# Folding the last four weight rows of the upper 64 partitions onto the lower 64, in the tail of a decode kernel

## Chip, cores and metric

The kernel runs on one core of one Trainium2 chip. The metric is the device time of one execution in microseconds (us). Before the change it is 829.26 us (median of 4 runs, 829.16 to 829.46), and most executions agree within 0.3 us, so differences of a few tenths of a per cent can be told apart. An engine below is either a compute engine, called by its name (PE is the matmul engine, DVE the vector engine, ACT the scalar engine, SP the one that issues the loads), or one of the core's 16 DMA engines, which move the loads.

## The reference

There are two decode attention blocks, A and B, with the same shapes, except that B looks only at the last 4096 keys. Their outputs are placed side by side.

```python
q = (x @ wq).reshape(B, Sq, 32, 128).transpose(0, 2, 1, 3)      # one query row, D = 512
scores = einsum("bhqd,bhkd->bhqk", q, k) * 128 ** -0.5          # A: 16384 keys, B: the last 4096
p = softmax(scores)
o = einsum("bhqk,bhkd->bhqd", p, v)
out = o.transpose(0, 2, 1, 3).reshape(1, 1, 4096) @ wo          # wo: 4096 x 512
# result: concatenate([out_A, out_B], axis=-1)
```

Keys and values are read once and used for one query, so the work is moving 352 MB from HBM.

## The kernel before

The change touches only the end: the loads of wo for block B and the matmuls that use them. wo has 4096 rows; partition p holds rows 32p to 32p + 31, so `wo_t` is 128 partitions x 32 rows x 512 columns in bf16, 1 KB a row. The attention output lies in `oc`, 128 partitions x 32 columns, in the same order. One output is then 32 matmuls that each contract 128 partitions (twice, because the 512 columns are cut in two).

```python
def _load_wo(nc, cx, st, j0, n):
    ...
    src = st.wo.rearrange("(p j) f -> p j f", j=J)              # J = 32
    cx.o(nc.sync.dma_start(out=st.wo_t[:, j0 : j0 + n, :], in_=src[:, j0 : j0 + n, :]))

def _out(nc, cx, st, j0, n):
    ...
    for j in range(j0, j0 + n):
        for x in range(2):
            cx.o(nc.tensor.matmul(out[x], lhsT=st.oc[:, j : j + 1],
                rhs=st.wo_t[:, j, x * w : (x + 1) * w], start=(j == 0), stop=(j == J - 1)))
    ... # at the end: cast to a row in SBUF (half on DVE, half on ACT), store

# the loads at the end of the queue, B's wo in shrinking pieces of 16, 8, 4, 2, 2 rows
pieces = [(stA, 0, J // 2), (stA, J // 2, J // 2)]
j0 = 0
for x in (J // 2, J // 4, J // 8, J // 16, J // 16):
    pieces.append((stB, j0, x))
    j0 += x
```

All large loads are issued by SP on one queue, in this order, and none is issued out of turn.

The softmax here doesn't subtract the row's maximum and nothing guards it: scores larger than these inputs give would overflow.

## Time and profile before

| | |
|---|---|
| time, median of 4 | 829.26 us |
| profiled execution | 829.14 us, of which the profile's span is 827.4 |
| DMA engines | at least 9 tenths busy in 39 of 40 slices |
| last landing of a load of woB | 824.36 us into the span |

The first lines are from the page of the kernel before: the span, the busy time of each compute engine with its share of the span, the busy tenths of the DMA engines in 40 slices, and a line of the DMA queue list (packets, MB, share).

```profile
span 827.4 us, 5769 instructions
...
PE 403.7 (49%) x2368; PEld 138.7 (17%) x2368; DVE 584.7 (71%) x286; ACT 68.1 (8%) x301; POOL 4.5 (1%) x17
...
DMA  9999999999999999999999999999999999999996
...
q8 instruction: 18, 0.29, 0.1%
```

DMA is the limit, and it is full from beginning to end. The q8 line: 18 packets of 16 KB are not data but instructions.

The end of the chain of waits of the kernel before (start, length, what; earlier steps are cut):

```profile
802.16 22.20 DMA woB<-in_B_wo_dram
824.36 0.04 issue
824.40 0.43 PE out L303 x4
824.83 0.41 DVE rowB L312
```

The last piece of woB, issued at 802.16, lands at 824.36; four matmuls and a cast follow, then the store. So the end of the program is the last landing and some 4.8 us (829.14 - 824.36).

The table by stretches of the kernel before (stretch in us, its length, busy us and, in brackets, instructions of PE, PEld (PE's loading of weights), DVE, ACT and POOL (the GpSimd engine, hardly used here), then the granted PE clock as a share of full speed, the busy share of the DMA engines, GB/s):

```profile
816.00:818.00 2.00, 1.58 (x16) 0.69 (x11) 0.40 (x2) 0.36 (x1) 0.00 (x0) 0.50 0.96 397
818.00:820.00 2.00, 0.63 (x12) 0.60 (x14) 0.11 (x2) 0.00 (x0) 0.00 (x0) 0.94 0.86 345
820.00:822.00 2.00, 1.44 (x28) 1.01 (x25) 0.00 (x0) 0.00 (x0) 0.00 (x0) 1.00 0.61 242
822.00:824.00 2.00, 1.72 (x28) 1.07 (x25) 0.00 (x0) 0.00 (x0) 0.00 (x0) 1.00 0.17 66
```

The rate does not fall to 0 at once; it fades from 397 to 66 GB/s between 816 and 824 us, while the busy share goes from 0.96 to 0.17. The trace has sixteen increments of its semaphore for each of these loads, spread over some 4.8 us. They are read here as one for each of the 16 DMA engines, raised when the engine is through with its part. That is the author's reading: no record names an engine. Wherever the text below speaks of early or late engines, or of what an engine does, it goes by it. By this reading the DMA engines stop one after the other. These are the increments, sorted, for two loads of woB before the change (worked out from the trace's semaphore records, us):

```
8-row piece      816.95 817.00 817.17 817.18 817.27 818.30 818.89 819.70 820.06 820.06 820.08 820.24 820.32 820.51 821.72 821.80
last 2-row piece 819.56 819.60 819.77 819.78 819.88 820.87 821.46 822.26 822.63 822.63 822.64 822.80 822.87 823.08 824.29 824.36
```

The first engine is through 4.8 us before the last one (819.56 and 824.36). This gap is what the change was after.

### The profile page before, as it was taken

To read this page: it belongs to the slowest core of one execution; us is meant where nothing else is said; L and a number is where in the kernel's file an instruction comes from. 1 tells how busy PE (TensorE), PEld (TensorE's weight loads), DVE (VectorE), ACT (ScalarE), POOL (GpSimd) and SP (SyncE) were. 2 spreads that over 40 slices of the span, in tenths; PEclk is the share of its full clock that TensorE was granted. 3 is DMA by queue.
4 is the path that set the end of the run, shared out by engine and by line. 5 is a ranking of instruction groups with operands and counts; after the bars stand their busy time and mean duration, and the time that the engine had idled before them with its cause. 6 is when DMAs were issued, how large, how long until landed. Compare 5 with 4: busy or idle time off the path is not lost.

```text
span 827.4 us, 5769 instructions
## 1 busy us (share of the span) xinstructions
PE 403.7 (49%) x2368; PEld 138.7 (17%) x2368; DVE 584.7 (71%) x286; ACT 68.1 (8%) x301; POOL 4.5 (1%) x17
## 2 busy tenths in 40 slices
PE   3356444434555544554454445445455455544355
PEld 1112111111211111211121111111111111211123
DVE  2892777777777777766777777777777776777760
ACT  2000011000100001000110001100010000100010
POOL 2000000000000000000000000000000000000000
PEclk9778677666776668766686666766677766676779
DMA  9999999999999999999999999999999999999996
GB/s 380 437 430 432 433 430 432 431 431 432 431 429 436 432 430 430 431 433 433 432 429 430 429 431 432 432 432 430 431 430 430 429 431 432 431 432 433 431 423 290
DMA packets 13902, 352.69 MB, mean 426 GB/s; under 512 B 2482, under 2 KB 2484, under 8 KB 2868
## 3 DMA queue, kind: packets, MB, share of 16 engines
q1 hardware_dynamic: 13588, 352.33, 99.2%
q8 instruction: 18, 0.29, 0.1%
q14 instruction: 8, 0.07, 0.0%
q10 hardware_dynamic: 288, 0.00, 0.0%
HBM read 352.32 MB, written 0.00 MB: 426 GB/s over the span
## 4 chain that ended last, share of the span: by engine, by line
DMA 68%; DVE 20%; issue 9%; PE 1%; SPq 1%; ACT 0%; DVEq 0%
DMA kt<-in_A_k_cache_dram 49%; DVE prod L161 12%; DMA kt<-in_B_k_cache_dram 12%; DVE half L173 6%; DMA wq_t<-in_B_wq_dram 3%; DMA woB<-in_B_wo_dram 3%; DMA vt<-in_B_v_cache_dram 2%; DVE sc L203 2%; SPq L154 1%; PE q_ps L123 1%; PE red L186 0%; PE acc L233 0%; ACT qallB L130 0%; DVEq L161 0%; DVE recip L267 0%
## 5 line engine op out<-in xcount | busy, mean ns | idle before, releaser
L186 PE MATMUL red<-half,ident 128*128 128x512 bf16 x640 | 253.3, 567 | 388.1 <-DVE half L173 374.4
L161 DVE TENSOR_TENSOR prod<-kt,qallA 128x8192 bf16<-128x8192 bf16 x64 | 283.2, 4426 | 159.8 <-DMA kt<-in_A_k_cache_dram 159.1
L173 DVE TENSOR_TENSOR half<-prod 128x4096 bf16<-128x4096 bf16 x80 | 182.5, 2282 | 0.0
L186 PEld LDWEIGHTS <-ident 128*128 128x128 bf16 x640 | 81.8, 128 | 535.3 <-issue 508.1
L161 DVE TENSOR_TENSOR prod<-kt,qallB 128x8192 bf16<-128x8192 bf16 x16 | 70.8, 4426 | 40.3 <-DMA kt<-in_B_k_cache_dram 40.1
L233 PE MATMUL acc<-vt,pA 128*16 128x512 bf16 x1024 | 89.4, 484 | 0.1
L210 ACT ACTIVATE pA<-sc 128x64 bf16<-128x64 f32 x64 | 16.4, 256 | 518.3 <-DVE sc L203 518.3
L203 DVE TENSOR_REDUCE sc<-red 128x64 f32<-128x512 f32 x80 | 54.7, 684 | 3.4 <-PE red L186 3.3
L233 PEld LDWEIGHTS <-pA 128*16 128x16 bf16 x1024 | 22.9, 100 | 73.2 <-issue 66.8
L210 ACT ACTIVATE p_sb<-sc,off 128x64 bf16<-128x64 f32 x64 | 21.5, 336 | 92.1 <-DVE sc L203 92.1
L257 PE MATMUL f_ps<-acc_sb,sel 128*4 128x128 f32 x128 | 16.6, 273 | 10.7 <-ACT acc_sb L244 10.7
L233 PE MATMUL acc<-vt,p_sb 128*16 128x512 bf16 x256 | 20.5, 450 | 0.2 <-DMA vt<-in_B_v_cache_dram 0.2
L244 ACT COPY acc_sb<-acc 128x512 f32<-128x512 f32 x16 | 9.4, 585 | 79.3 <-PE acc L233 79.3
L123 PE MATMUL q_ps<-wq_t,xbA 128*128 128x512 bf16 x32 | 8.5, 431 | 13.2 <-DMA wq_t<-in_A_wq_dram 13.2
L257 PEld LDWEIGHTS f_ps<-acc_sb,sel 128*4 128x4 f32 x128 | 9.8, 86 | 14.5 <-ACT acc_sb L244 12.3
L210 ACT ACTIVATION_READ_ACCUMULATOR pA<-sc 128x1 f32 x64 | 11.9, 187 | 0.0
L210 ACT ACTIVATION_READ_ACCUMULATOR p_sb<-sc,off 128x1 f32 x64 | 11.9, 187 | 0.0
L123 PE MATMUL q_ps<-wq_t,xbB 128*128 128x512 bf16 x32 | 7.2, 379 | 2.3 <-DMA wq_t<-in_B_wq_dram 1.6
L233 PEld LDWEIGHTS <-p_sb 128*16 128x16 bf16 x256 | 5.4, 95 | 15.6 <-issue 13.1
L269 ACT ACTIVATE orow<-f_ps,recip 4x128 bf16<-4x128 f32 x16 | 5.7, 358 | 20.5 <-DVE recip L267 20.5
L95 DVE COPY xbB<-xTB 128x32 bf16<-128x32 bf16 x16 | 1.5, 199 | 8.1 <-DMA xTB<-in_B_x_dram 8.1
L267 DVE RECIPROCAL recip<-f_ps 4x1 f32<-4x1 f32 x16 | 2.4, 150 | 6.0 <-PE f_ps L257 6.0
(35 smaller groups left out, 53.6 us busy)
## 6 DMA issues: line engine op xcount, KB each, us to landing
kt<-in_A_k_cache_dram SPq DMA_DIRECT2D x32, 4096.0 KB, 27.1
vt<-in_A_v_cache_dram SPq DMA_DIRECT2D x32, 4096.0 KB, 29.6
kt<-in_B_k_cache_dram SPq DMA_DIRECT2D x32, 1024.0 KB, 23.7
vt<-in_B_v_cache_dram SPq DMA_DIRECT2D x32, 1024.0 KB, 22.5
wq_t<-in_A_wq_dram SPq DMA_DIRECT2D x1, 4096.0 KB, 12.4
wq_t<-in_B_wq_dram SPq DMA_DIRECT2D x1, 4096.0 KB, 23.8
woA<-in_A_wo_dram SPq DMA_DIRECT2D x2, 2048.0 KB, 29.3
woB<-in_B_wo_dram SPq DMA_DIRECT2D x1, 2048.0 KB, 23.6
```

The lines of the kernel that those rows point to most:

```text
L123: cx.o(nc.tensor.matmul(q_ps[:, :], lhsT=st.xb[:, c, g, :], rhs=w[:, g, j * (512 // DH) : (j + 1) * (512 // DH), :], start=(g == 0 and c = ...
L154: cx.o(nc.sync.dma_start(out=t[g:P:n, :, :], in_=src))
L161: cx.o(nc.vector.tensor_tensor(out=ch.prod[:, :, :], in0=u.kt[:, ch.k0 : ch.k0 + U, :], in1=q.rearrange("p (o d) -> p o d", o=1).broadcast ...
L173: cx.o(nc.vector.tensor_tensor(out=ch.half[:, :, :], in0=ch.prod[:, :, 0 : DH // 2], in1=ch.prod[:, :, DH // 2 : DH], op=ALU.add,))
L186: cx.o(nc.tensor.matmul(ch.red[:, :, :], lhsT=cx.ident[:, :], rhs=ch.half[:, :, b * W : (b + 1) * W], start=(b == 0), stop=(b == nb - 1),))
L203: cx.o(nc.vector.tensor_reduce(out=sc[:, :], in_=ch.red[:, :, :], axis=AX.X, op=ALU.add))
L210: cx.o(nc.scalar.activation(out=ch.p[:, :, g, :], in_=sc[:, :].rearrange("p (t e) -> p t e", e=4), func=ACT.Exp, scale=SCALE, bias=0.0 if ...
L233: cx.o(nc.tensor.matmul(gr.acc[r : r + 4 * G, :], lhsT=ch.p[:, t, :, :], rhs=u.vt[:, k : k + 4, :], start=(first and t < 4), stop=(last an ...
L244: cx.o(nc.scalar.copy(gr.acc_sb[:, :], gr.acc[:, :]))
L257: cx.o(nc.tensor.matmul(gr.f_ps[:, 0:DH], lhsT=cx.sel[:, e, :], rhs=gr.acc_sb[:, e * DH : (e + 1) * DH], start=False, stop=(e == 3), skip_ ...
L267: cx.o(nc.vector.reciprocal(recip[:, :], gr.f_ps[:, DH : DH + 1]))
L269: cx.o(nc.scalar.activation(out=gr.orow[:, :], in_=gr.f_ps[:, 0:DH], func=ACT.Copy, scale=recip[:, 0:1]))
```

## The change

The intent was to even out the finish. The change rests on a guess that no trace had shown: that the late DMA engines are those that bring the rows of the upper partitions, so that some of these rows are better sent to the lower ones. The last four rows of each of the partitions 64 to 127 go into a second tile, `wo_f`, on partitions 0 to 63, and are multiplied there. That needs the upper half of four columns of `oc` on the lower partitions (`ocf`), which a matmul with a slice of the identity and a copy on DVE bring there. The pieces of woB are now 16, 8, the fold (4 rows as two loads of 64 partitions), 2 and 2.

```diff
+LO = 0
+FOLD = 4
+def _load_wo_folded(nc, cx, st):
+    J = st.wo.shape[0] // P
+    st.wo_f = cx.half_pool.tile([P, FOLD, st.DN], BF16, tag="half", name="wo_f")
+    src = st.wo.rearrange("(p j) f -> p j f", j=J)[:, J - FOLD :, :]
+    to = st.wo_t[LO : LO + P // 2, J - FOLD :, :]
+    cx.o(nc.sync.dma_start(out=to, in_=src[LO : LO + P // 2, :, :]))
+    far = P // 2 - LO
+    to = st.wo_f[LO : LO + P // 2, :, :]
+    cx.o(nc.sync.dma_start(out=to, in_=src[far : far + P // 2, :, :]))
...  # in _out, for the folded piece only (own = partitions 0 to 63)
+        ocf_ps = cx.oc_ps[own, 256 : 256 + n]
+        cx.o(nc.tensor.matmul(
+            ocf_ps, lhsT=cx.ident[:, far : far + P // 2], rhs=st.oc[:, j0 : j0 + n], ...))
+        st.ocf = cx.singles.tile([P, n], BF16, tag="ocf", name="ocf")
+        cx.o(nc.vector.tensor_copy(st.ocf[own, :], ocf_ps))
...
-                lhsT=st.oc[:, j : j + 1],
-                rhs=st.wo_t[:, j, x * w : (x + 1) * w],
+                lhsT=st.oc[own, j : j + 1],
+                rhs=st.wo_t[own, j, x * w : (x + 1) * w],
+            if own.stop - own.start < P:
+                cx.o(nc.tensor.matmul(out[x], lhsT=st.ocf[own, j - j0 : j - j0 + 1],
+                    rhs=st.wo_f[own, j - j0, x * w : (x + 1) * w], start=False, stop=False))
...
+    pieces += [(stB, J - FOLD, FOLD), (stB, J - 2 * FOLD, FOLD // 2)]
+    pieces += [(stB, J - 2 * FOLD + FOLD // 2, FOLD // 2)]
```

The bytes moved are the same; there is one load more, and PE gets one placing matmul and 8 matmuls more.

More of the change, by code (lines that the diff above doesn't have):

```diff
@@ L289, in _fin_col, with _out @@
     cx.oc_first = False
-def _out(nc, cx, st, j0, n):
+def _out(nc, cx, st, j0, n, last=False):
     J = st.wo.shape[0] // P
@@ L298, in _out @@
         cx.o(nc.vector.tensor_copy(st.oc[:, :], cx.oc_ps[:, st.oc_at : st.oc_at + J]))
+    own = slice(LO, LO + P // 2) if n == FOLD and j0 == J - FOLD else slice(0, P)
+    if own.stop - own.start < P:
+        far = P // 2 - LO
+        ocf_ps = cx.oc_ps[own, 256 : 256 + n]
+        cx.o(nc.tensor.matmul(
+            ocf_ps, lhsT=cx.ident[:, far : far + P // 2], rhs=st.oc[:, j0 : j0 + n],
+            start=True, stop=True, skip_group_check=True,
+        ))
+        st.ocf = cx.singles.tile([P, n], BF16, tag="ocf", name="ocf")
+        cx.o(nc.vector.tensor_copy(st.ocf[own, :], ocf_ps))
     w = st.DN // 2
@@ L304, in _out @@
                 out[x],
-                lhsT=st.oc[:, j : j + 1],
-                rhs=st.wo_t[:, j, x * w : (x + 1) * w],
+                lhsT=st.oc[own, j : j + 1],
+                rhs=st.wo_t[own, j, x * w : (x + 1) * w],
                 start=(j == 0),
-                stop=(j == J - 1),
+                stop=(last and j == j0 + n - 1),
             ))
-    if j0 + n == J:
+            if own.stop - own.start < P:
+                cx.o(nc.tensor.matmul(
+                    out[x],
+                    lhsT=st.ocf[own, j - j0 : j - j0 + 1],
+                    rhs=st.wo_f[own, j - j0, x * w : (x + 1) * w],
+                    start=False,
+                    stop=False,
+                ))
+    if last:
         row = cx.singles.tile([1, st.DN], BF16, tag=f"row{st.name}", name=f"row{st.name}")
@@ L469 @@
             ld.add("vt", lambda u=units[i - 1]: _load_kv(nc, cx, u, "v"))
-    pieces = [(stA, 0, J // 2), (stA, J // 2, J // 2)]
-    j0 = 0
-    for x in (J // 2, J // 4, J // 8, J // 16, J // 16):
-        pieces.append((stB, j0, x))
-        j0 += x
+    pieces = [(stA, 0, J // 2), (stA, J // 2, J // 2), (stB, 0, J // 2), (stB, J // 2, J // 4)]
+    pieces += [(stB, J - FOLD, FOLD), (stB, J - 2 * FOLD, FOLD // 2)]
+    pieces += [(stB, J - 2 * FOLD + FOLD // 2, FOLD // 2)]
     for p in pieces:
-        ld.add(None if p[1] else "kt", lambda p=p: _load_wo(nc, cx, *p))
+        if p == (stB, J - FOLD, FOLD):
+            ld.add(None, lambda: _load_wo_folded(nc, cx, stB))
+        else:
+            ld.add(None if p[1] else "kt", lambda p=p: _load_wo(nc, cx, *p))
     _load_x(nc, cx, stA)
@@ L532 @@
     for p in pieces:
-        _out(nc, cx, *p)
+        _out(nc, cx, *p, last=(p in (pieces[1], pieces[-1])))
 _INS = ['A_x', 'A_k_cache', 'A_v_cache', 'A_wq', 'A_wo', 'B_x', 'B_k_cache', 'B_v_cache', 'B_wq', 'B_wo']
```

## The prediction

> **What bounds the kernel.** The page shows the 16 DMA engines busy 9 tenths in 39 of 40 slices, at about 430 GB/s; DVE has 71%, PE 49%. The chain of waits ends with woB landing 22.20 us after its issue at 802.16, then four matmuls (0.43 us from 824.40) and the rowB casts (0.41 us). Only what happens after about 815 us can move the end; the load stream before is untouched.
>
> **The tail before.** [...] These increments in the trace show the last 2-row piece of woB landing between 819.56 and 824.36 us. This spread is 0.6 us at 32 us and grows in steps of about 1.2 us. The DMA queue list has 18 instruction packets of 16 KB (q8; about 1.1 us each). Eight engines seem to take them (two or three each) and are 3.1 to 4.8 us behind the first; the other eight 0 to 2.7 us. That the late eight serve partitions 64 to 127 is an inference: no record names an engine.
>
> **What the change does.** It moves 64 x 4 KB = 256 KB of destinations from upper to lower partitions, in the piece before the last two. [...] If that holds for a 64-partition load, the late eight are relieved of 32 KB each, 1.22 us by the median 32 KB packet: the last landing moves to about 823.5, set by an early engine that got more. [...] then no engine's bytes change and the last landing stays at 824.4. No run here shows which; I give each about half.
>
> **What PE adds.** One placing matmul, one DVE copy and 8 more 256-column matmuls. In the timeline 32 such matmuls take 1.91 us and 16 take 1.04: 0.054 us each plus 0.2 of latency. The round trip PE, DVE, PE costs about 0.5 us (ocA: 809.33 to 809.85). It stands in program order after the 8-row piece, whose landing (821.80) the change does not move, being queued ahead of the fold. So PE ends at 821.84 + 16 x 0.054 + 0.5 + 16 x 0.054 + 8 x 0.054 + 0.2 = 824.7 us, against 824.83 now. PE becomes the tail's limit, so most of the 0.9 us that DMA might gain is not seen: 0.1 to 0.2 us earlier if engines are relieved, unchanged to 0.2 later if not. One more DMA issue (0.33 us) is hidden: loads are queued over 20 us ahead, and wo_f's slot is free by then.
>
> **Predicted time.** 829.1 us, 8 times in 10 between 828.4 and 829.8. Faster by over 2%: 0.3%; within 2%: 99.4%; slower by over 2%: 0.3%.
>
> **What would show it.** In the timeline of the last 10 us the 8-row woB matmuls still start near 821.8; then placing matmul and ocf copy, PE idle about 0.4 us; then the rest nearly back to back, with the last out matmul ending near 824.7. If engines were relieved, the last landing is near 823.5 and the first about 1.2 us later than before; if not, 824.4, and PE waits again for the last piece. Everything before 800 us: same.
>
> **What would make it wrong.** The 18 extra PE instructions cause another instruction fetch, late, on a late engine (1.2 us); the 64-partition loads run slower than 128-partition ones (about 1 us); the half slot delays the last DVE chunk; or the late engines are those of the lower partitions, so the last landing moves to about 825.6.

"These increments" are the sixteen increments above, read as one for each engine; "if that holds" is the inference at the end of the paragraph before, that the late eight bring the rows of the upper partitions; "then no engine's bytes change" is the other branch, in which a load of 64 partitions is spread over all sixteen engines. Both branches were guesses, half and half. The sum for PE comes to 824.7 us, 0.1 us before the 824.83 of the kernel before, hence the 829.1 us.

## The result

The time after the change is 832.45 us (median of 4 runs, 832.13 to 833.70) against 829.26 us before. The ratio is 1.0041 (95% interval 1.0026 to 1.0056). Ratios here are the mean time of one kernel's runs over that of the other's runs of the same rounds, so not quite the ratio of the medians. The change costs 3.2 us. By a limit of 2% that is "the same", but it is far outside the noise and outside the predicted range.

The profiled execution after the change happens to be the slowest of the four (833.70); this is kept in mind below. From its page, the span and the DMA line:

```profile
span 831.9 us, 5789 instructions
...
DMA  9999999999999999999999999999999999999995
```

The end of the chain of waits after the change (earlier steps are cut):

```profile
795.81 28.44 DMA woB<-in_B_wo_dram
824.25 0.04 issue
824.29 1.87 PE out L327 x16
826.16 0.14 PE oc_ps L317
826.30 0.30 PE out L327
826.60 0.31 PE out L335
...
828.41 0.99 PE out L327 x8
829.41 0.41 DVE rowB L344
```

The first line is the surprise. The load that the chain goes back to is the 8-row piece, which stands in the queue ahead of the fold, and which the prediction took as untouched. It landed at 821.80 before and at 824.25 now. After it the chain is PE: 5.1 us up to the cast, where the prediction had 2.9.

The same stretches after the change:

```profile
816.00:818.00 2.00, 1.49 (x15) 0.68 (x10) 0.48 (x2) 0.36 (x1) 0.00 (x0) 0.50 0.98 262
818.00:820.00 2.00, 0.00 (x0) 0.08 (x1) 0.03 (x1) 0.00 (x0) 0.00 (x0) 0.99 0.99 264
820.00:822.00 2.00, 1.36 (x22) 1.00 (x23) 0.00 (x0) 0.00 (x0) 0.00 (x0) 0.87 0.78 215
822.00:824.00 2.00, 1.47 (x14) 0.79 (x11) 0.00 (x0) 0.00 (x0) 0.00 (x0) 0.50 0.66 167
824.00:826.00 2.00, 1.71 (x16) 0.86 (x15) 0.00 (x0) 0.00 (x0) 0.00 (x0) 0.50 0.27 89
```

The DMA engines are as busy as before from 816 to 818 (0.98 against 0.96), but they move 262 GB/s instead of 397. So a packet takes longer, as its records show below. (A packet here is the part of a load that goes to one partition: the trace has 128 packets of 4 KB for the four rows of 128 partitions.) The increments and the packet durations say the same (from the trace; the fold is the first of its two loads):

```
after, 8-row piece      816.82 816.87 816.91 817.17 817.22 819.66 820.55 821.38 821.48 821.62 821.80 821.91 821.92 821.98 824.07 824.25
after, fold, 1st load   818.09 818.13 818.18 818.40 818.57 820.90 821.62 822.48 822.59 822.70 822.78 822.94 823.04 823.28 824.88 825.34
after, last 2-row piece 820.70 820.80 820.93 821.43 822.27 824.08 824.47 824.84 824.91 825.00 825.19 825.25 825.26 826.00 826.79 827.38

packets after 812 us, median and longest, ns    before        after
4 KB (before: the 4-row piece; after: the fold)   159, 169      249, 494
8 KB (the 8-row piece, 128 partitions)            312, 321      386, 639
```

Three things are read from this. First, all sixteen engines seem to take part in each load of the fold: it has sixteen increments, and every one comes at least 0.8 us after the corresponding one of the piece ahead, in sorted order. So the fold is read as spread over all sixteen, and nothing shows an engine relieved of bytes. Second, the earliest five engines need 1.2 to 1.4 us for a load of 16 KB each (an even share of its 256 KB), twice what 16 KB take elsewhere (0.61 us for a 16 KB packet). Third, the slowdown reaches loads that were not changed: 8 KB packets of the 8-row piece took up to 639 ns, twice the usual 312, at a time when the early engines had started on the fold while the late ones were still at that piece. The 8-row piece lost 2.45 us in this way (821.80 to 824.25), and the last landing 3.0 us in all (824.36 to 827.38). Even the 16-row piece, two places ahead of the fold, landed later: at 820.60 instead of 819.33.

The PE clock adds to it in this one execution. The matmuls of woB after the change, from the timeline:

```profile
820.64 2.83 PE L327 MATMUL out<-woB,ocB 128*1 128x256 bf16 x32 [3.15 <-DMA woB<-in_B_wo_dram]
824.29 1.87 PE L327 MATMUL out<-woB,ocB 128*1 128x256 bf16 x16 [0.82 <-DMA woB<-in_B_wo_dram]
828.35 1.01 PE L327 MATMUL out<-woB,ocB 128*1 128x256 bf16 x8
```

and from that of the kernel before:

```profile
819.37 1.91 PE L303 MATMUL out<-woB,ocB 128*1 128x256 bf16 x32 [1.79 <-DMA woB<-in_B_wo_dram]
821.84 1.04 PE L303 MATMUL out<-woB,ocB 128*1 128x256 bf16 x16 [0.56 <-DMA woB<-in_B_wo_dram]
824.40 0.38 PE L303 MATMUL out<-woB,ocB 128*1 128x256 bf16 x4 [0.27 <-DMA woB<-in_B_wo_dram]
```

Sixteen matmuls took 1.87 us instead of 1.04, at a granted clock of 0.50 instead of 1.00 in those stretches. So this execution ended in PE, 6.3 us after the last landing (833.70 - 827.38) instead of 4.8. The other three runs, 832.13 to 832.49, have no profile; they would fit a last landing near 827.5 and 4.8 us after it, but that is only arithmetic.

### The profile page after: what moved, and what is told of

It reads as the page before. It is cut to its first block, busy times and chain, and to the rows that moved or that the text cites. A ratio compares the mean times of both kernels' runs of the same rounds, so it can differ in the third digit from the quotient of the medians.

```text
span 831.9 us, 5789 instructions
## 1 busy us (share of the span) xinstructions
PE 406.3 (49%) x2377; PEld 140.6 (17%) x2377; DVE 584.8 (70%) x287; ACT 68.2 (8%) x301; POOL 4.6 (1%) x17
## 4 chain that ended last, share of the span: by engine, by line
DMA 66%; DVE 22%; issue 10%; SPq 1%; PE 1%; DVEq 0%; ACTq 0%
DMA kt<-in_A_k_cache_dram 48%; DVE prod L175 13%; DMA kt<-in_B_k_cache_dram 12%; DVE half L187 6%; DMA woB<-in_B_wo_dram 3%; DMA xTB<-in_B_x_dram 3%; DVE sc L217 2%; SPq L168 1%; PE out L327 0%; DVE xbB L97 0%; PE out L335 0%; DVEq L175 0%; DVE recip L281 0%; DVE rowB L344 0%; ACTq L90 0%
## 5 line engine op out<-in xcount | busy, mean ns | idle before, releaser
L247 PE MATMUL acc<-vt,pA 128*16 128x512 bf16 x1024 | 86.5, 471 | 0.0
L327 PE MATMUL out<-woB,ocB 128*1 128x256 bf16 (+1 forms) x64 | 7.7, 380 | 4.0 <-DMA woB<-in_B_wo_dram 4.0
```

The costliest lines, as they stand in the source:

```text
L247: cx.o(nc.tensor.matmul(gr.acc[r : r + 4 * G, :], lhsT=ch.p[:, t, :, :], rhs=u.vt[:, k : k + 4, :], start=(first and t < 4), stop=(last an ...
L327: cx.o(nc.tensor.matmul(out[x], lhsT=st.oc[own, j : j + 1], rhs=st.wo_t[own, j, x * w : (x + 1) * w], start=(j == 0), stop=(last and j == ...
```

## The experiments

Theory 1, formed on this result: what costs is where the fold's bytes are written, all of them on partitions 0 to 63. At first this theory also guessed that the late engines are the ones that write these partitions. Theory 2: a load of 64 partitions is slow as such. Theory 3: PE's extra work costs the time. Each experiment below ran with three timed rounds beside the kernel before on the same chip, except the fourth, which is one look.

### 1. The fold mirrored

```diff
-LO = 0
+LO = 64
```

> The fold mirrored: LO = 64, so the last 4 rows of partitions 0 to 63 go onto 64 to 127 and are multiplied there; as many loads, bytes and instructions as in the change. Theory 1 (the late engines are those that write partitions 0 to 63, and the fold makes the early engines write there too, while the late ones are still at it): the 8-row piece lands at 821.8 again, the last landing is 824.1 to 824.8, and the time is 829.0 to 830.0. Theory 2 (a 64-partition load is slow on whichever half): as the change, last landing near 827, 832 to 832.7. Theory 3 (the extra PE work costs the time): as the change, 832 to 832.7, though the last landing would be early.

Measured: 834.96 us (834.24 to 835.56), before 829.27, ratio 1.0068 (1.0053 to 1.0083). The 8-row piece landed at 826.10 and the last piece at 829.40. No theory expected this. The mirrored fold is slower still, so the idea of theory 1 that the lower half was simply the wrong one to choose has fallen. The four runs lie in two pairs, 834.3 and 835.6; the profiled one is of the slower pair, and its matmuls from 828 us on ran at a granted clock of 0.50.

### 2. Two half loads without a fold

Each half goes to its own partitions; PE works as before the change.

```diff
-    to = st.wo_f[LO : LO + P // 2, :, :]
-    cx.o(nc.sync.dma_start(out=to, in_=src[far : far + P // 2, :, :]))
+    for p0 in (LO, P // 2 - LO):
+        own = slice(p0, p0 + P // 2)
+        cx.o(nc.sync.dma_start(out=st.wo_t[own, J - FOLD :, :], in_=src[own, :, :]))
```

> The four rows are loaded by two 64-partition loads, each onto its own partitions (0 to 63 first, then 64 to 127), nothing is folded and PE works as before the change. Theory 1: half of the change's extra writes to the lower partitions, so the last landing moves by 0.4 to 1.5 us (824.8 to 825.9), time 829.7 to 830.8. Theory 2: as the change, last landing near 827, 832 or so. Theory 3 (PE): 829.3, as before the change.

Measured: 832.43 us (832.24 to 832.62), ratio 1.0038 (1.0023 to 1.0053), last landing 827.55. This is the whole cost of the change, and the fold is not in it. It is enough that four rows come as a lower and an upper half. The size that theory 1 gave (829.7 to 830.8) was wrong; theory 2 gave the right one. The stretches are the ones to compare with experiment 11:

```profile
816.00:818.00 2.00, 0.83 (x8) 0.33 (x5) 0.51 (x2) 0.36 (x1) 0.00 (x0) 0.50 0.94 293
818.00:820.00 2.00, 0.00 (x0) 0.00 (x0) 0.00 (x0) 0.00 (x0) 0.00 (x0) 0.50 1.00 264
```

### 3. PE's part alone

The four rows come by one 128-partition load; PE does the placing matmul, the copy and the 16 half matmuls, with rows at hand in place of `wo_f`. Its output is wrong, which doesn't matter for the time.

```diff
-            ld.add(None, lambda: _load_wo_folded(nc, cx, stB))
+            ld.add(None, lambda p=p: _load_wo(nc, cx, *p))
-                    rhs=st.wo_f[own, j - j0, x * w : (x + 1) * w],
+                    rhs=st.wo_t[own, j, x * w : (x + 1) * w],
```

> PE's part alone: the four rows come by one 128-partition load as before the change; PE does the placing matmul, the copy and the 16 half matmuls, with rows at hand as a stand-in for the folded ones (wrong result on purpose). Theories 1 and 2: landings as before the change (last 824.4), time 829.1 to 829.8. Theory 3: 832 or so.

Measured: 829.95 us (828.82 to 830.20), ratio 1.0005 (0.9989 to 1.0022), last landing 824.10. Theory 3 is out. The spread is wider than elsewhere. In the profiled run (829.78) PE sets the end, and the stretches show why (same columns as above):

```profile
820.00:822.00 2.00, 2.00 (x26) 1.19 (x23) 0.00 (x0) 0.00 (x0) 0.00 (x0) 0.58 0.60 235
822.00:824.00 2.00, 2.00 (x20) 0.96 (x18) 0.15 (x1) 0.00 (x0) 0.00 (x0) 0.56 0.11 42
```

PE is busy all the time, at a clock of 0.58 and 0.56, where the kernel before had 1.00. The tail's PE work thus shows by up to about 1 us in a run (830.20 against 829.27) and not at all in another (828.82). That the clock makes this difference is likely but not shown, because the stretches of the other three runs are not on record.

### 4. Which engines are late

The kernel before, with four small loads onto 8, 4, 2 and 1 partitions put between the last loads.

```diff
+def _mark(nc, cx, st, k):
+    t = cx.singles.tile([P, 256], BF16, tag=f"mark{k}", name=f"mark{k}")
+    cx.o(nc.sync.dma_start(out=t[0:k, :], in_=st.wo[0:k, 0:256]))
...
+        if i < 4:
+            ld.add(None, lambda k=8 >> i: _mark(nc, cx, stB, k))
```

> The kernel before with four small extra loads of 512 B rows in the tail, onto 8, 4, 2 and 1 partitions. [...] Theory 1: the 8 landings of the first fall among the late landings of the load queued ahead of it (3.1 to 4.9 us behind the first of that load). [...] The time: same as before the change within 0.5 us.

Measured: 829.10 us in its one run (of unknown state, as a single run is). The marks raise their semaphores once at the issue and then 8, 4, 2 and 1 times, which fits one increment for each engine that takes part. The 8-partition mark beside the load queued ahead of it (from the trace, us; each increment of the mark has one of that load about 0.2 us before it, and is taken to be of the same engine):

```
load ahead  799.88 800.06 800.07 800.09 800.12 801.14 801.38 802.68 802.77 802.86 802.98 803.06 803.10 803.24 803.28 804.70
mark of 8   800.10 800.26 800.30 801.33 801.58 802.88 803.07 803.19
```

Three of the eight are among the five early engines, two are the middle ones, and three are among the nine late ones. Theory 1 had all eight among the late ones. So, by the reading of the increments, the engines that write partitions 0 to 7 in this small load are neither all late nor all early, and the guess of theory 1 about who is late finds no support. Nothing here ties the late engines to one half of the partitions, as the change had assumed.

Theory 1 is left with its core, now called theory A: what costs is that the partitions of one load lie together, in one half or less. It needs no word on who is late. Theory B is that splitting a load costs, whichever partitions it takes. The kernel before holds a hint: its loads of the B caches go to 32 partitions each, every fourth one, and run at the full rate: the page has 429 to 437 GB/s in its slices 2 to 38, in which they take their turns with those of A, and the last four of them, 1 MB each, land 2.28 to 2.44 us apart.

### 5 and 6. The same four loads, strided or in blocks

Both replace the fold by four loads of 32 partitions onto their own partitions. They differ in one line, and have the same number of loads, bytes and 4 KB packets.

```diff
+    for g in range(4):
+        own = slice(g, P, 4)                    # 5: every fourth partition
+        own = slice(32 * g, 32 * g + 32)        # 6: blocks of 32
+        cx.o(nc.sync.dma_start(out=st.wo_t[own, J - FOLD :, :], in_=src[own, :, :]))
```

> The four rows come by four loads of 32 partitions each, every fourth partition (0, 4, 8 and so on, then 1, 5, 9), each row onto its own partition; PE as before the change. In the trace of the kernel before, 32-partition loads of this form (the B cache) run at the full rate. Theory A (what costs is that one load's partitions lie together [...]): no cost, 829.0 to 829.8, 4 KB packets near 160 ns. Theory B (splitting a 128-partition load into loads of fewer partitions costs, whichever they are): slower than the two halves, 832.4 or more.

> The same four loads of 32 partitions, but of contiguous blocks (0 to 31, 32 to 63, 64 to 95, 96 to 127), each row onto its own partition; PE as before the change. Same number of loads, bytes and packets as the strided ones. Theory A: [...] as slow as the halves: 831.5 to 833.5, many 4 KB packets of 250 to 350 ns. Theory B: the same time as the strided loads, whatever that is.

Measured: strided 829.14 us (829.06 to 829.28), ratio 0.9997 (0.9982 to 1.0011); blocks 832.53 us (832.00 to 832.83), ratio 1.0037 (1.0022 to 1.0051). The stretches of the strided loads and then of the blocks:

```profile
816.00:818.00 2.00, 0.32 (x6) 0.10 (x3) 0.51 (x2) 0.36 (x1) 0.00 (x0) 1.00 0.94 391
818.00:820.00 2.00, 0.53 (x10) 0.44 (x11) 0.00 (x0) 0.00 (x0) 0.00 (x0) 1.00 0.86 347
```

```profile
816.00:818.00 2.00, 1.13 (x12) 0.49 (x7) 0.51 (x2) 0.36 (x1) 0.00 (x0) 0.50 1.01 305
818.00:820.00 2.00, 0.00 (x0) 0.00 (x0) 0.00 (x0) 0.00 (x0) 0.00 (x0) 0.50 0.94 253
```

The strided loads move 391 and 347 GB/s, as before the change (397 and 345), with 4 KB packets of 159 ns in the median and 169 at most. The blocks move 305 and 253, with packets up to 445 ns. Last landings are 824.48 and 827.40. Only the choice of partitions differs, so that is the cause, and theory B has fallen. One thing changes with it, though: a load that names other partitions also reads other rows of wo from HBM. These runs do not part the two sides. Two facts speak for the writing side. A load of a B cache reads one unbroken 1 MB and still runs at the full rate (the 2.28 to 2.44 us above), onto every fourth partition; and the mirrored fold reads the same two sets of rows as the change, in the other order, and lands its last piece 2.0 us later (829.40 against 827.38).

### 7. The loads of the change without PE's part

```diff
-        ocf_ps = ...            # the placing matmul and the copy of ocf
-            if own.stop - own.start < P:
-                ...             # the 8 matmuls on wo_f
```

The result is wrong on purpose.

> The loads of the change with PE's extra work taken out: no placing matmul, no copy, no matmuls on the folded rows (wrong result on purpose); the 8 half matmuls of the lower partitions stay. If the loads alone cost the time (theories A and B): last landing near 827.4 as in the change, time 831.4 to 832.5. If PE's work costs a good part: 830.5 or less.

Measured: 832.53 us (832.30 to 832.57), ratio 1.0037 (1.0022 to 1.0052), against 832.45 for the whole change. The end of its chain of waits:

```profile
804.80 23.01 DMA woB<-in_B_wo_dram
827.81 0.04 issue
827.85 0.43 PE out L318 x4
828.27 0.41 DVE rowB L327
```

The loads alone cost all of it, and the chain has the form of the kernel before, 3.45 us later (827.81 against 824.36).

### 8. The placing matmul early

The placing matmul and the copy of `ocf` stand right after the copy of `ocB`.

```diff
+    if j0 == 0 and st.name == "B":
+        lo = slice(LO, LO + P // 2)
+        ...                     # placing matmul and copy of ocf, moved here
```

> The change, with the placing matmul and the copy of ocf moved to right after the copy of ocB, some 6 us before they are needed, so the round trip PE, DVE, PE leaves the tail. If the last landing sets the end, as theories A and B have it, 832.0 to 832.5, at most 0.4 us better than the change. If PE's chain after the 8-row piece sets the end: 0.4 to 0.6 us better, 831.8 to 832.1.

Measured: 831.96 us (831.86 to 832.19), ratio 1.0031 (1.0014 to 1.0047), last landing 827.27. That is 0.5 us better than the change by the medians of two different jobs, but the intervals of the ratios overlap, and experiment 7, with still less work on PE, is not better than the change. The profiles say where that 0.5 us lies: the last landing is 0.54 us earlier than in experiment 7 (827.27 against 827.81), as the time is (832.01 against 832.54). What the round trip costs stays open between 0 and 0.5 us; it is at most a sixth of the loss.

### 9 and 10. Place and dose

Experiment 9 queues the two half loads of experiment 2 ahead of the rest of woB. Experiment 10 leaves them in place and brings the 8-row piece by halves too, so 1.5 MB come by halves instead of 0.5 MB.

```diff
 # 9
+        if p == (stB, 0, J // 2):
+            ld.add("kt", lambda: _load_wo_folded(nc, cx, stB))     # the two halves, then the piece
 # 10
+            h = p == (stB, J // 2, J // 4)                         # this piece in two halves
+            ld.add(None if p[1] else "kt", lambda p=p, h=h: _load_wo(nc, cx, *p, halves=h))
```

> The two half loads of the second experiment (each onto its own partitions, no fold), but queued ahead of the rest of woB instead of behind its 8-row piece, so that every engine has at least 200 KB left to move after them. [...] 831.5 to 833. If it costs only where engines are running out of work: 829.2 to 830.

> The dose: the 8-row piece also comes by two half loads, each onto its own partitions, so 1.5 MB instead of 0.5 MB of halves; PE as before the change. If it is the halves that cost, time grows with their bytes: two half loads of 4 rows cost 3.1 us, of which at least 1.2 us is the own doubled time of 32 KB per engine, so 12 rows should cost at least 3.6 us: 833.5 to 838.5. If the cost is a fixed one of having half loads in the queue: 832 to 832.8.

In the expectation of experiment 9, the range 831.5 to 833 is for a cost that comes wherever the half loads stand.

Measured: experiment 9 took 834.79 us (834.70 to 835.28), ratio 1.0066 (1.0049 to 1.0083), last landing 828.83. That is worse than the highest figure expected (833): the cost is not one of the tail alone, and farther ahead it is larger, not smaller. One part is visible. The first half load, which only brings 16 KB to each engine if shared evenly, was landed between 810.76 and 819.40, the 16-row piece behind it at 825.05 instead of 819.33, and PE then had nearly all of woB to do, 63 matmuls in 5.93 us, so that the run ended 6.5 us after its last landing. Why the landings themselves are 1.3 us later than those of experiment 2 was not tested.

Experiment 10 took 835.00 us (834.63 to 835.21), ratio 1.0068 (1.0053 to 1.0083), last landing 830.54. The last landing is 3.2 us late with 0.5 MB of halves and 6.2 us late with 1.5 MB. The cost grows with the bytes that come by halves, though less than in proportion.

### 11. Even and odd partitions

This is experiment 2 with one line changed: 64 partitions a load, but every second one.

```diff
-    for p0 in (LO, P // 2 - LO):
-        own = slice(p0, p0 + P // 2)
+    for p0 in (0, 1):
+        own = slice(p0, P, 2)
```

> As the second experiment, two loads of 64 partitions each onto their own partitions, in the same place of the queue, but the even partitions first and then the odd ones, instead of the lower half and then the upper. Number of loads, rows, bytes and packets are equal. If what costs is that one load's partitions all lie in one half: no cost, 829.0 to 829.8, 4 KB packets near 160 ns. If a 64-partition load costs whichever partitions it takes (and the 32-partition strided loads escaped by their size): as the halves, 832 to 832.8.

Measured: 829.26 us (829.23 to 829.42), ratio 1.0000 (0.9984 to 1.0017), last landing 824.50, 4 KB packets 159 ns in the median and 169 at most. Its stretches, beside those of experiment 2:

```profile
816.00:818.00 2.00, 1.13 (x12) 0.49 (x7) 0.51 (x2) 0.36 (x1) 0.00 (x0) 0.50 0.94 391
818.00:820.00 2.00, 0.49 (x6) 0.32 (x7) 0.00 (x0) 0.00 (x0) 0.00 (x0) 0.50 0.87 350
```

Beside experiment 2 (832.43) this leaves nothing but which 64 partitions a load names, and with them the rows of wo that it reads.

The profiled executions together, last landing of woB and time in us:

| kernel | last landing | time of the profiled run | time less landing |
|---|---|---|---|
| before | 824.36 | 829.14 | 4.8 |
| even, odd (11) | 824.50 | 829.26 | 4.8 |
| strided (5) | 824.48 | 829.08 | 4.6 |
| PE alone (3) | 824.10 | 829.78 | 5.7, PE sets the end |
| marks (4) | 824.41 | 829.10 | 4.7 |
| halves (2) | 827.55 | 832.31 | 4.8 |
| blocks (6) | 827.40 | 832.00 | 4.6 |
| loads alone (7) | 827.81 | 832.54 | 4.7 |
| placing early (8) | 827.27 | 832.01 | 4.7 |
| the change | 827.38 | 833.70 | 6.3, PE sets the end |
| halves ahead (9) | 828.83 | 835.28 | 6.5, PE sets the end |
| the fold mirrored (1) | 829.40 | 835.56 | 6.2, PE sets the end |
| more halves (10) | 830.54 | 835.21 | 4.7 |

No version beat the kernel before; the best, strided loads, equals it.

## Why the prediction was wrong

**What bounds the kernel, and the tail before.** Right. DMA is the limit, the end follows the last landing, and the sixteen engines finish 4.8 us apart, by the reading of the increments. That instruction packets make them late fits the 18 packets of about 1.1 us and the steps of 1.2 us (the spread is 0.62 us at 51.5 us and 1.87 at 61.2, and the first such packet starts at 56.2), but no run tested it.

**"That the late eight serve partitions 64 to 127 is an inference."** Not supported: in experiment 4 a load onto partitions 0 to 7 has three of its eight increments among the late ones. It had no part in the result, because of the next point.

**Engines relieved, or no engine's bytes changed, about half each.** Each load of the fold has sixteen increments in step with those of the load before, which is read as all sixteen used. By that the prediction's second branch was the right one here.

**"Then no engine's bytes change and the last landing stays at 824.4."** This is the step that failed. The bytes per engine do stay, as far as the sixteen increments show, but the time per byte does not. The prediction costed the fold's 32 KB per engine by the 1.22 us of a packet of a 128-partition load, and in this branch added nothing. In the runs, 4 KB packets of half loads took 249 ns in the median and up to 494, against 159; the engines were busy and moved 262 GB/s instead of 397. The prediction named slower 64-partition loads among the things that would make it wrong, with a guess of 1 us; they cost 3.0 us of landing. One microsecond is about what the early engines lose: the first landing moved from 819.56 to 820.70, 1.1 us. The last engine loses more, and most of it before its own fold: it was 2.45 us late at the 8-row piece, while the early engines' fold packets ran beside it, and 3.0 us late at the end. That the last landing of each load belongs to one and the same engine is assumed here; no record names it.

**"whose landing (821.80) the change does not move, being queued ahead of the fold".** Wrong for this reason: 824.25. The first increment of the fold came at 818.09, 6.2 us before the last one of the piece ahead of it (824.25). So loads that stand behind one another in the queue run at the same time, and by the reading of the increments on different engines.

**What PE adds.** About right as a sum at full clock: in experiment 8, where two matmuls took 0.11 us as they do at a clock of 1.00 (experiment 3 from 824 us), the 23 matmuls after the landing of the fold's second load took 1.61 us (826.12 to 827.73), where the prediction has 1.5 for 24. In the change the round trip took 0.46 us (placing matmul at 826.09, first use of `ocf` at 826.55) for 0.5 predicted. It was not seen in the median time: the loads alone give 832.53, the whole change 832.45. What was missing is that the clock in the tail can be 0.5, which makes the same matmuls 0.8 us longer for sixteen.

**The hidden risks.** Neither another instruction packet (18 before and after) nor the half slot played a part: experiment 2 loses as much without using that slot.

Shown: the cost comes with the loads, not with PE (3, 7); it comes from which partitions, and so which rows of wo, one load names, not from their number nor from the number of loads (2 and 11, 5 and 6); it grows with the bytes (10). Not shown: by what mechanism. That engines share something on the writing side when the partitions of one load lie together is the author's guess. 16 KB in twice the usual time on the first five engines (1.2 to 1.4 us against 0.61) would fit two engines that take turns, but packets of up to three times the usual length (494 against 159 ns) are more than that would give, no record names anything that is shared, and the reading side was not varied alone. Open: why the mirrored fold is worse by 2.5 us in the median, of which the last landing shows 2.0; this was not tested.

## What to carry to other kernels

Before a load is split or moved to other partitions, look at which partitions one load names, not only at its bytes: a set that spreads evenly over all 128, such as every second or fourth, kept the full rate here (829.26 and 829.14 us, against 829.26 before), while contiguous halves or quarters cost 3 us for half a megabyte (832.43 and 832.53); in the change, such loads slowed an unchanged one running beside them (its 8 KB packets took up to 639 ns instead of 312). A rate that falls while the DMA engines stay busy, with packets well over their usual length (here 249 against 159 ns in the median), is the sign; the rate was 262 GB/s instead of 397 at a busy share of 0.98. And a queue position did not shield a load here (821.80 to 824.25 for the 8-row piece): read all the increments of the loads before taking one ahead in the queue as untouched.
